# First chunk's heads: more idle products, one pair's softmax split over GpSimd and one exponential, the first weight's scaling placed earlier

## Chip, cores, metric

One core of a Trainium2 chip. The metric is the device time of one execution in microseconds (us); lower is better.

## What is computed

Attention over 8 batches, 8 heads, 576 positions and 64 dimensions, then a two-layer feed-forward block on the 4608 tokens. Heads 0 to 3 are local (a query sees the 32 keys up to its own position), heads 4 to 7 are strided (keys at the same position modulo 32).

```python
scores = scale * q @ k.T
scores = where(mask, scores, -1e9)
attn = exp(scores - max(scores)); attn /= sum(attn) + 1e-9
x = (attn @ v) -> [4608, 512]
h = maximum(x @ w_in, 0)            # w_in  [512, 2048]
out = (h * h) @ w_out               # w_out [2048, 512]
```

## The kernel before

The 4608 tokens go through in 12 chunks of 384. For each chunk TensorE does 16 steps of `up` (line 465: x times a slice of w_in, 12 products of 384 columns) and 16 steps of `down` (line 493: squared result times a slice of w_out, 9 products of 512 columns). To keep single precision, every operand is split into a high and a low part and three products stand for one.

**The start.** Before the first `up` the x of chunk 0 has to be there. Its eight heads are worked on in four pairs by `pe_pair` (line 295), a generator that the main code advances step by step: `first[0]` and `first[1]` are the two pairs of local heads, `late[0]` and `late[1]` the two pairs of strided ones. A pair goes through scores on TensorE (line 325), masked row minima on VectorE (line 330), exponentials on ScalarE, row sums and reciprocals on VectorE (lines 358, 359), the multiplication by the reciprocal (line 362), transposes on TensorE into the banks of the scores (line 368), copies to SBUF (lines 370, 372), the products with v (lines 380, 391), and the split into the x tiles (lines 395, 396).

**Two ways to the exponential.** The local pairs of chunk 0 (`single`) take eight exponentials of 128 columns, each with its own bias and row sum (line 353), from SBUF into the PSUM bank of the scores; ScalarE reads its accumulator out after each. All other pairs subtract the minima on GpSimd (line 355), take one exponential per head (line 356) and sum on VectorE (line 357).

**Idle products.** `zeros(bank, n)` issues n products of 128 columns whose result nobody reads: 60 at the very start, 45 after the scores of the first three pairs. The products of `first[0]` with v are issued three times over (line 378), to the same place. 12 more stand ahead of the first `down`.

**The weights.** `convert` (line 147) is a generator over the 16 weight blocks, in two halves each: a scaling of the raw block on ScalarE (`scale`, line 154), a step on ScalarE into PSUM bank 3 (line 166), one on VectorE (line 169), a copy of the high part on ScalarE (line 172) and a subtraction for the low part on GpSimd (line 173). `behind(ins, gen)` puts each instruction that gen issues behind the given instruction of the same engine. The first two steps are placed behind the last exponential of `first[1]`; the four that follow stand behind the last copy of the heads (line 395), and the others are spread between the `up` steps of chunk 0.

**Order.** The framework's planner places the traced instructions on each engine by its own estimate of time, with the order of the trace as priority; the engines then take them strictly in that order. While chunk 0 runs through `up` and `down`, GpSimd and VectorE also do chunk 1's strided heads by elementwise multiplications and reductions (`strided`, line 400), which begin behind the fifth weight subtraction.

Of the kernel before, what the change touches and what calls it, by code (L numbers as in the profile page):

```python
# [11 lines left out]
AF = mybir.ActivationFunctionType  # L12
ALU = mybir.AluOpType
AX = mybir.AxisListType
# [14 lines left out]
QC = 96  # L29
NW = TC // QC  # L30
# [8 lines left out]
NWARM = 60  # L39
# [10 lines left out]
def f32(ap):  # L50
    return ap.bitcast(F32)
# [11 lines left out]
def windows(c):  # L63

    res, at = [], 0
    for b, g in SEGS[c]:
        for qc in (2 * g, 2 * g + 1):
            if res and res[-1][:2] != (b, qc - 1):
                at += STR
            res.append((b, qc, at))  # L70
            at += QC
    return res
# [14 lines left out]
def attn_moe(ctx: ExitStack, tc, qk_l, v_l, qk_d, v_d, qk_p, v_p, f_s, q_s, k_s, v_s, w_in, w_out, masks, eye, out):  # L87
    nc = tc.nc
# [13 lines left out]
    def psum(i, nm):  # L102

        return ps.tile([P, 512], F32, name=nm, tag=f"ps{i}")
# [17 lines left out]
    last = {}  # L122
# [9 lines left out]
    def fetch(k):  # L132

        p, which = order[k]
        src = (w_out if which else w_in)[p].bitcast(U32).rearrange("p (n t) -> p n t", t=2)
        if k < 12:
            raw = wpool.tile([P, 1024, 2], U32, name=f"raw{k}", tag=f"w{k + 8 if k < 8 else k + 4}")
            nc.sync.dma_start(out=raw, in_=src)
            raws[k] = [(raw, slice(0, 1024))]
        else:  # L140
            raws[k] = []
            for i in range(0, 1024, WP):
                raw = spool.tile([P, WP, 2], U32, name=f"raw{k}_{i}", tag="s3", bufs=5)
                nc.sync.dma_start(out=raw, in_=src[:, i : i + WP])
                raws[k].append((raw, slice(i, i + WP)))

    def convert():

        split = None

        def scale(k):
            for raw, _ in raws[k]:

                nc.scalar.activation(f32(raw[:, :, 1]), f32(raw[:, :, 1]), AF.Prelu, scale=2.0**-112, alpha=-(2.0**32))  # L154

        scale(0)
        for k in range(NFT):
            p, which = order[k]
            t = wpool.tile([P, 2, 1024], F32R, name=f"w{which}_{p}", tag=f"w{k}")
            (wo if which else wi)[p] = t[:, 0], t[:, 1]  # L160
            cuts = [(raw[:, i : i + WP], sl.start + i) for raw, sl in raws.pop(k) for i in range(0, sl.stop - sl.start, WP)]
            for raw, at in cuts:

                z = psum(zbank[next(zturn) % len(zbank)], f"z{k}_{at}").bitcast(U32)
                w, hi, lo = raw[:, :, 1], t[:, 0, at : at + WP], t[:, 1, at : at + WP]
                first_step = nc.scalar.activation(z, raw[:, :, 0], AF.Copy, bias=-0.49, scale=2.0**-29 * (1 - 2.0**-9))  # L166
                if split:
                    split()
                last["v"] = nc.vector.scalar_tensor_tensor(out=w, in0=w, scalar=3, in1=z, op0=ALU.logical_shift_left, op1=ALU.bitwise_or)

                def split(w=w, hi=hi, lo=lo, at=at, k=k):
                    last["a"] = nc.scalar.copy(hi, f32(w))
                    last["g"] = nc.gpsimd.tensor_sub(lo, f32(w), f32(hi))  # L173
                    if at and 4 <= k < 12:
                        fetch(k + 4)

                if k == 0 and at:
                    split()
                    split = None
                if not at and k + 1 < NFT and k + 1 in raws:  # L180
                    with tc.issue_after(first_step.ins):
                        scale(k + 1)
                yield
        split()
# [110 lines left out]
    def pe_pair(c, pr, local, qk, vr, es, pt, banks, sm, single):  # L295
# [3 lines left out]
        if local:  # L299
            kw, wins, nv = KW, [at for _, _, at in windows(c)], P  # L300
            src, vsrc = qk_d[c, pr], v_d[c, pr]
            mk = [mask_sb[:QC, w % 2, :] for w in range(NW)]
        else:
            kw, wins, nv = QC, [QC * w for w in range(NW)], QC
# [9 lines left out]
        nm = small.tile([P, 2, NW], F32, name=f"nm{u}", tag="nm")  # L314
        rs = small.tile([P, 2, NW], F32, name=f"rs{u}", tag="rs")
        ss = sums[sm]
# [3 lines left out]
        e4 = [blocks(e) for e in es]  # L320

        r4 = [blocks(t) for t in s_ps] if single else e4
# [23 lines left out]
                minima(h, s)  # L346
        yield
        for h in range(2):
            if single:
                for w in range(NW):  # L350
                    if c == 0 and pr and h and not w:
                        yield
                    last["a"] = nc.scalar.activation(r4[h][:, w], e4[h][:, w], AF.Exp, bias=nm[:QC, h, w : w + 1], scale=-1.0, accum_out=ss[:QC, NW * h + w, :1])  # L353
            else:
                nc.gpsimd.tensor_sub(e4[h], e4[h], nm[:QC, h].unsqueeze(2).broadcast_to([QC, NW, kw]))  # L355
                last["a"] = nc.scalar.activation(e4[h], e4[h], AF.Exp, scale=-1.0)
                nc.vector.tensor_reduce(out=ss[:QC, NW * h : NW * (h + 1), 0], in_=e4[h], op=ALU.add, axis=AX.X)
        nc.vector.tensor_reduce(out=rs[:QC].rearrange("p h w -> p (h w)"), in_=ss[:QC], op=ALU.add, axis=AX.X)
        last["v"] = nc.vector.reciprocal(rs[:QC], rs[:QC])
# [4 lines left out]
        p4 = pt.rearrange("p (h w q) -> p h w q", h=2, w=NW)  # L364
        for h in range(2):
            t = s_ps[h] if s_ps else banks()
            for w in range(NW):
                nc.tensor.transpose(t[:kw, w * QC : (w + 1) * QC], e4[h][:, w], ident[:QC, :QC])
            if c == 0 and not local:
                nc.vector.tensor_copy(pt[:kw, h * TC : (h + 1) * TC], t[:kw, :TC])  # L370
            else:
                last["a"] = nc.scalar.copy(pt[:kw, h * TC : (h + 1) * TC], t[:kw, :TC])
# [148 lines left out]
    def behind(ins, gen):  # L521

        while True:
            with ExitStack() as st:
                for i in ins.values():
                    st.enter_context(tc.issue_after(i.ins))
                try:
                    k = next(gen)
                except StopIteration:
                    return  # L530
            yield k


    def pair_at(c, pr, local, place, psum_at):
        u = f"{c}_{pr}_{int(local)}"
        buf = lambda pl, nm, n, tag, **kw: pl.tile([P, n], F32, name=f"{nm}{u}", tag=tag, **kw)
        ee = lambda pl, tag: [buf(pl, f"e{h}", 512, tag) for h in range(2)]
        if place == 0:
            b = buf(lraw, "qk", TC + KC, "qk"), buf(lpool, "v", 512, "vx", bufs=1), ee(lpool, "e"), buf(lpool, "pt", 2 * TC, "px")
        elif place == 1:  # L540
            b = buf(lraw, "qk", TC + KC, "qk"), buf(ypool, "v", 512, "ysb"), ee(ypool, "ysb"), buf(lpool, "pt", 2 * TC, "px")
        elif place == 2:
            e = buf(xpool, "e", 2 * TC, "xlh")
            b = buf(xpool, "qk", 2 * TC, "xll"), buf(xpool, "v", 2 * TC, "xsl")[:, :512], [e[:, :TC], e[:, TC:]], buf(lpool, "pt", 2 * KC, "kx", bufs=1)[:, : 2 * TC]
        else:

            t = buf(wpool, "w", 2048, "w7")
            b = buf(xpool, "qk", 2 * TC, "xsh"), buf(spool, "v", 512, "s3", bufs=5), [t[:, :512], t[:, 512:1024]], t[:, 1024 : 1024 + 2 * TC]
        it = iter(range(10))

        def bank():
            i = next(it) % len(psum_at)
            if psum_at[i] == "y":
                return ps_y.tile([P, 512], F32, name=f"b{i}{u}", tag="psy")
            return psum(int(psum_at[i]), f"b{i}{u}")

        return pe_pair(c, pr, local, *b, bank, place % 3, c == 0 and local)
# [21 lines left out]
    def take(c, which):  # L579

        if NPLAIN <= c < NCHUNK:
            for h in map(int, which):
                if (c, h) not in heads:
                    heads[c, h] = pe_head(c, h)
                with ExitStack() as st:
# [4 lines left out]
                    last["pe"] = last.get("mm", last["pe"])  # L590

    ungated = convert()

    late = [pair_at(0, pr, False, 2 + pr, ("y0", "14")[pr]) for pr in range(2)]
# [7 lines left out]
    def zeros(bank, n):  # L602
        w_ps = psum(bank, f"w_ps{bank}")
        for _ in range(n):
            nc.tensor.matmul(w_ps[:, :P], warm, warm, start=True, stop=True)  # L605
# [17 lines left out]
        for k in range(NEARLY, 8):  # L623
            fetch(k)
    next(late[0])
    zeros(1, 3 * NWARM // 4)
    next(first[0])
    parts = last["v"], last["a"]
    with tc.issue_after(parts[1].ins):
# [4 lines left out]
    next(first[0])  # L634
    with tc.issue_after(last["a"].ins):
        next(first[1])
    weights = behind({"a": last["a"]}, ungated)
    next(first[1])
    next(late[1])
    for _ in range(2):  # L640
        next(weights)
    next(first[0])
# [4 lines left out]
    weights = behind({"a": last["a"]}, ungated)  # L647
# [6 lines left out]
    for s in range(NS + 2):  # L654
        c, j = divmod(s, NFT)
# [19 lines left out]
        if s < NFT - 2:  # L675

            weights = behind({"a": last["gh"]} | ({"x": last["xs"]} if s > NFT - 4 else {}), ungated)
# [108 lines left out]
```

## Time and profile before

| | us |
|---|---|
| median of 3 runs | 880.89 |
| lowest, highest | 880.71, 881.80 |
| profiled execution, its time | 881.58 |
| profiled execution, its span | 879.8 |
| outside the span | 1.8 |
| mean granted TensorE clock | 0.998 |

| engine | busy us | share of the span |
|---|---|---|
| TensorE | 869.2 | 99% |
| VectorE | 640.5 | 73% |
| ScalarE | 571.7 | 65% |
| GpSimd | 672.4 | 76% |

These shares are means over unlike stages: the start (up to 27.5 us), the `up` and `down` of chunk 0 beside the conversion of the weights (to 108 us), and eleven chunks in which TensorE has all it needs. In the views, PE is TensorE's products, PEld its weight loads, DVE VectorE, ACT ScalarE, POOL GpSimd.

### The profile page before, as it was taken

The page shows a single profiled execution, that of the slowest core. Times are in us where ns is not written, and L with a number is a line of the kernel's source. Part 1 is how long each engine was busy: PE and PEld are TensorE (multiplying, and loading weights), DVE is VectorE, ACT ScalarE, POOL GpSimd, SP SyncE. Part 2 cuts the span into 40 slices and gives each one's busy share as a digit, 9 for nine tenths or more (in the row PEclk, how much of TensorE's full clock was granted, in tenths as well). Part 3 has the DMA queues.
Part 4 walks back from the last instruction along what each step waited for, and adds up shares of the span by engine and source line. Part 5 has one row for each costly group of instructions (what it writes and reads, how often), then busy time and mean ns, then how long its engine had stood idle before and what let it go on. Part 6 is the DMA issues. An engine that isn't in the chain of part 4 may idle for free.

```text
span 879.8 us, 14906 instructions
## 1 busy us (share of the span) xinstructions
PE 869.2 (99%) x4773; PEld 790.0 (90%) x4773; DVE 640.5 (73%) x1900; ACT 571.7 (65%) x1506; POOL 672.4 (76%) x718
## 2 busy tenths in 40 slices
PE   8999999999999999999999999999999999999997
PEld 7788899999999999999999999999998989999996
DVE  5796687787787887878878778878787787883111
ACT  6999777586676566657657758657666665664332
POOL 3589778877988989888988978997998899782000
PEclk9999999999999999999999999999999999999999
DMA  9853531323123023112202302312131121000000
GB/s 356 356 199 107 163 101 39 101 84 113 31 78 111 26 89 103 44 51 85 67 13 80 115 13 74 97 38 75 31 102 57 32 71 61 6 1 12 26 1 36
DMA packets 26798, 71.41 MB, mean 81 GB/s; under 512 B 2976, under 2 KB 8736, under 8 KB 25184
## 3 DMA queue, kind: packets, MB, share of 16 engines
q1 hardware_dynamic: 26432, 70.14, 24.0%
q8 instruction: 37, 0.61, 0.3%
q14 instruction: 41, 0.34, 0.1%
q10 hardware_dynamic: 288, 0.33, 0.1%
HBM read 61.01 MB, written 9.44 MB: 80 GB/s over the span
## 4 chain that ended last, share of the span: by engine, by line
PE 90%; POOL 4%; ACT 2%; DVE 1%; DMA 1%; issue 1%; DVEq 0%; POOLq 0%; ACTq 0%
PE y L508 42%; PE h L475 42%; POOL w L173 2%; PE s L237 2%; PE o L283 2%; DMA raw<-w_out 1%; PE w_ps L605 1%; PE b L380 1%; ACT b L353 1%; ACT raw L154 1%; ACT z L166 0%; POOL pp L447 0%; DVE sc L432 0%; PE b L391 0%; POOL e L355 0%
## 5 line engine op out<-in xcount | busy, mean ns | idle before, releaser
L508 PE MATMUL y<-w,gh 128*128 128x512 f32 x1152 | 357.9, 391 | 0.5 <-POOL w L173 0.5
L508 PEld LDWEIGHTS y<-w,gh 128*128 128x128 f32 x1152 | 212.7, 188 | 40.5 <-POOL w L173 0.8
L475 PE MATMUL h<-xlh,w 128*128 128x384 f32 x768 | 229.1, 339 | 1.4 <-ACT xlh L395 0.9
L447 POOL TENSOR_TENSOR pp<-vs,sc 128x448 f32<-128x448 f32 (+10 forms) x192 | 189.9, 1013 | 48.9 <-DVE qs L448 23.0
L475 PE MATMUL h<-xsh,w 128*128 128x384 f32 x768 | 226.3, 335 | 0.3 <-POOL w L173 0.3
L508 PE MATMUL y<-w,gl 128*128 128x512 f32 x576 | 225.2, 392 | 0.0
L425 POOL TENSOR_TENSOR pq<-ks,qs 128x512 f32<-128x512 f32 (+2 forms) x192 | 197.7, 1050 | 18.6 <-DVE sc L426 13.2
L489 DVE TENSOR_TENSOR gl<-h,gh 128x384 fp32r<-128x384 f32 x192 | 105.5, 550 | 80.9 <-ACT gh L488 79.6
L488 ACT CAST gh<-h 128x384 fp32r<-128x384 f32 x192 | 91.3, 476 | 104.4 <-PE y L508 103.0
L486 ACT ACTIVATE h<-h 128x384 f32<-128x384 f32 x176 | 83.1, 472 | 110.0 <-PE h L475 109.5
L426 DVE TENSOR_REDUCE sc<-pq 128x8 f32<-128x512 f32 (+4 forms) x228 | 119.7, 534 | 45.3 <-POOL pq L425 42.6
L475 PEld LDWEIGHTS h<-xlh,w 128*128 128x128 f32 x768 | 141.3, 188 | 5.0 <-ACT xlh L395 1.1
L475 PEld LDWEIGHTS h<-xsh,w 128*128 128x128 f32 x768 | 141.4, 188 | 1.1 <-POOL w L173 0.6
L475 PE MATMUL h<-xll,w 128*128 128x384 f32 x384 | 129.0, 336 | 0.0
L508 PEld LDWEIGHTS y<-w,gl 128*128 128x128 f32 x576 | 108.1, 188 | 22.9
L475 PE MATMUL h<-xsl,w 128*128 128x384 f32 x384 | 128.3, 334 | 0.0
L448 DVE TENSOR_REDUCE qs<-pp 128x64 f32<-128x448 f32 (+11 forms) x192 | 106.4, 562 | 27.2 <-POOL pp L447 25.2
L487 ACT ACTIVATE h<-h 128x384 f32<-128x384 f32 x176 | 83.2, 473 | 3.6
L262 DVE STREAM_TRANSPOSE p_t<-e 32x128 f32<-32x128 f32 x240 | 72.3, 301 | 11.2 <-ACT e L251 6.6
L475 PEld LDWEIGHTS h<-xll,w 128*128 128x128 f32 x384 | 72.2, 188 | 2.4 <-DVE xll L396 0.3
L475 PEld LDWEIGHTS h<-xsl,w 128*128 128x128 f32 x384 | 72.1, 188 | 0.1
L246 ACT ACTIVATE e<-e,nm 96x128 f32<-96x128 f32 x160 | 62.5, 392 | 10.0 <-DVE nm L229 8.7
(101 smaller groups left out, 1077.2 us busy)
## 6 DMA issues: line engine op xcount, KB each, us to landing
qk<-qk_l SPq DMA_DIRECT2D x24, 400.0 KB, 3.2
y<-ysb SPq DMA_DIRECT2D x36, 256.0 KB, 3.5
raw<-w_in SPq DMA_DIRECT2D x7, 1024.0 KB, 10.9
qk<-qk_l SPq DMA_DIRECT2D x16, 416.0 KB, 3.2
vs<-v_s SPq DMA_DIRECT2D x10, 576.0 KB, 3.8
raw<-w_out SPq DMA_DIRECT2D x5, 1024.0 KB, 12.6
v<-v_l SPq DMA_DIRECT2D x40, 128.0 KB, 2.0
ks<-k_s SPq DMA_DIRECT2D x8, 576.0 KB, 3.7
```

Of the source, the lines that this page charges most:

```text
L246: nc.scalar.activation(e[:QC, cut(w)], e[:QC, cut(w)], AF.Exp, bias=nmax[:QC, w : w + 1], scale=-1.0, accum_out=ssum[:QC, w, :1])
L262: nc.vector.transpose(out=pt[STR * k : STR * (k + 1), :, STR * r : STR * (r + 1)], in_=e.rearrange("p (w k) -> p w k", k=KW)[STR * r : STR ...
L425: nc.gpsimd.tensor_mul(pv, kt[:, a : a + m, :], qt[:, i - i0 : i - i0 + 1, :].broadcast_to([P, m, D]))
L426: nc.vector.tensor_reduce(out=sc[:, i - i0, a : a + m], in_=pv, op=ALU.add, axis=AX.X)
L447: nc.gpsimd.tensor_mul(pv, vt[:, a : a + nd, :n], sc[:, il : il + 1, :n].broadcast_to([P, nd, n]))
L448: nc.vector.tensor_reduce(out=ot[:, il, a : a + nd], in_=pv, op=ALU.add, axis=AX.X)
L475: done = nc.tensor.matmul(ph[:, :TC], w[:, wsl], xx, start=n == 0, stop=n == 11)
L486: nc.scalar.activation(g, g, AF.Relu)
L487: nc.scalar.activation(g, g, AF.Square)
L488: last["gh"] = nc.scalar.copy(gh, g)
L489: nc.vector.tensor_sub(gl, g, f32(gh))
L508: done = nc.tensor.matmul(y_ps[c][t], g[:, sl], w[:, wsl], start=j == 0 and k == 0, stop=j == NFT - 1 and k == 2)
```

## The change

It does five things. (1) The second group of idle products has 55 instead of 45. (2) The four transposes of the second head of `first[0]` are issued twice, to the same place. (3) The second head of `first[1]` no longer takes four exponentials with accumulators: GpSimd subtracts the minima from all 512 columns, ScalarE takes one exponential of 512 columns into the PSUM bank, VectorE sums the rows out of it. (4) The scaling of the first weight block becomes a step of its own (a `yield` behind it), traced behind that exponential and ahead of the transposes of `first[1]` and the rest of `late[1]`. (5) The first two conversion steps proper are traced after that rest and stand behind `late[1]`'s first exponential on ScalarE (remembered as `a0`) and its last reciprocal on VectorE.

```diff
@@ convert
         scale(0)
+        yield
         for k in range(NFT):
@@ pe_pair
         for h in range(2):
-            if single:
+            if single and pr and h:
+
+                yield
+                nc.gpsimd.tensor_sub(e4[h], e4[h], nm[:QC, h].unsqueeze(2).broadcast_to([QC, NW, kw]))
+                last["a"] = nc.scalar.activation(r4[h], e4[h], AF.Exp, scale=-1.0)
+                nc.vector.tensor_reduce(out=ss[:QC, NW * h : NW * (h + 1), 0], in_=r4[h], op=ALU.add, axis=AX.X)
+            elif single:
                 for w in range(NW):
-                    if c == 0 and pr and h and not w:
-                        yield
                     last["a"] = nc.scalar.activation(r4[h][:, w], e4[h][:, w], AF.Exp, bias=nm[:QC, h, w : w + 1], scale=-1.0, accum_out=ss[:QC, NW * h + w, :1])
             else:
                 nc.gpsimd.tensor_sub(e4[h], e4[h], nm[:QC, h].unsqueeze(2).broadcast_to([QC, NW, kw]))
                 last["a"] = nc.scalar.activation(e4[h], e4[h], AF.Exp, scale=-1.0)
+                last["a0"] = last["a0" if h else "a"]
@@ pe_pair, transposes
-            for w in range(NW):
+
+            for w in [*range(NW)] * (2 if c == 0 and local and not pr and h else 1):
                 nc.tensor.transpose(t[:kw, w * QC : (w + 1) * QC], e4[h][:, w], ident[:QC, :QC])
@@ main
-    zeros(1, 3 * NWARM // 4)
+    zeros(1, NWARM - 5)
@@ main
     with tc.issue_after(last["a"].ins):
         next(first[1])
-    weights = behind({"a": last["a"]}, ungated)
+    next(behind({"a": last["a"]}, ungated))
     next(first[1])
     next(late[1])
+    weights = behind({"a": last["a0"], "v": last["v"]}, ungated)
     for _ in range(2):
         next(weights)
```

## Rows read from the trace of the kernel before

**Rows 1.** The page's chain that ended last, shares of the span by line.

```profile
PE y L508 42%; PE h L475 42%; POOL w L173 2%; PE s L237 2%; PE o L283 2%; DMA raw<-w_out 1%; PE w_ps L605 1%; PE b L380 1%; ACT b L353 1%; ACT raw L154 1%; ACT z L166 0%; POOL pp L447 0%; DVE sc L432 0%; PE b L391 0%; POOL e L355 0%
```

**Rows 2.** The same chain in order of time (start, length, what), the start.

```profile
15.97 4.22 PE b L380 x48
...
21.17 1.29 DVE e L362 x2
...
27.61 0.47 ACT xsh L395
```

**Rows 3.** Busy time by stretch: length, PE, PEld, DVE, ACT, POOL, clock, DMA share, GB/s.

```profile
14.00:16.00 2.00, 1.07 (x9) 0.76 (x9) 2.00 (x10) 2.00 (x8) 0.26 (x1) 1.00 1.03 430
16.00:18.00 2.00, 2.00 (x24) 1.82 (x26) 1.96 (x14) 1.63 (x7) 1.49 (x2) 0.63 1.00 410
18.00:20.00 2.00, 2.00 (x28) 2.00 (x24) 1.11 (x6) 2.00 (x6) 1.72 (x3) 0.51 1.01 422
20.00:22.00 2.00, 1.68 (x17) 1.22 (x17) 1.30 (x3) 2.00 (x4) 1.61 (x2) 1.00 1.04 422
22.00:24.00 2.00, 1.86 (x30) 1.58 (x30) 2.00 (x5) 1.51 (x4) 0.00 (x0) 1.00 0.98 410
...
32.00:36.00 4.00, 3.60 (x27) 2.84 (x26) 2.67 (x6) 4.00 (x8) 1.62 (x2) 1.00 1.03 407
```

**Rows 4.** TensorE in order of time, products and weight loads: start, length, what, [idle before].

```profile
9.86 2.69 PE L605 MATMUL w_ps<-p_t 128*128 128x128 bf16 x45
12.47 1.33 PE L325 MATMUL b<-qk 64*96 64x96 f32 x16
...
15.04 0.37 PEld L368 LDWEIGHTS b<-ident,e 96*128 96x128 f32 x4 [0.28 <-ACT e L356]
...
16.34 3.66 PEld L380 LDWEIGHTS b<-pt,v 128*64 128x64 f32 x46 [0.18 <-ACT pt L372]
...
25.24 0.69 PEld L380 LDWEIGHTS b<-pt,v 128*64 128x64 f32 x14
```

**Rows 5.** VectorE in order of time, the start.

```profile
15.30 0.24 DVE L330 CUSTOM_DVE_ANT_0 w<-b,mask_sb 96x96 f32<-96x96 f32 x1
...
18.90 0.55 DVE L357 TENSOR_REDUCE sums<-w 96x4 f32<-96x384 f32 x1 [0.77 <-ACT w L356]
...
20.70 0.55 DVE L370 COPY pt<-b 96x384 f32<-96x384 f32 x1 [0.81 <-PE b L368]
...
27.46 1.22 DVE L396 TENSOR_TENSOR xsl<-b,xsh 64x384 fp32r<-64x384 f32 x2
```

**Rows 6.** GpSimd in order of time.

```profile
12.66 1.61 POOL L355 TENSOR_TENSOR e<-e,nm 96x384 f32<-96x384 f32 x2 [9.81 <-DVE nm L330]
...
18.12 1.61 POOL L362 TENSOR_TENSOR e<-e,rs 96x384 f32<-96x384 f32 x2
...
45.09 5.21 POOL L173 TENSOR_TENSOR w<-raw,w 128x512 fp32r<-128x512 f32 x4
```

**Rows 7.** ScalarE in order of time, the start.

```profile
17.45 0.35 ACT L353 ACTIVATE b<-e,nm 96x128 f32<-96x128 f32 x1
...
17.96 0.37 ACT L353 ACTIVATE b<-e,nm 96x128 f32<-96x128 f32 x1
...
19.16 1.11 ACT L154 ACTIVATE raw<-raw 128x1024 f32<-128x1024 f32 x1
```

**Rows 8.** Lines by form, least/median/most ns (356, 357); landing of the first two weight loads.

```profile
L356 ACT ACTIVATE e<-e x6: 508/614/632, 14.2 to 79.5; 96x512 f32<-96x512 f32 x4, 96x384 f32<-96x384 f32 x2
...
L357 DVE TENSOR_REDUCE sums<-e x6: 539/676/684, 14.8 to 80.1; 96x4 f32<-96x512 f32 x4, 96x4 f32<-96x384 f32 x2
...
DMA to landing us min/median/max: 8.8/9.8/10.9
```

**Rows 9.** VectorE and TensorE in order of time, while chunk 0 runs.

```profile
47.07 3.29 DVE L432 TENSOR_TENSOR sc<-sc,mx 128x36 f32<-128x36 f32 x1
...
103.77 0.62 PE L475 MATMUL h<-xlh,w 128*128 128x384 f32 x2 [0.91 <-ACT xlh L395]
```

## The prediction

> **What bounds the kernel now.** I read the page's chain by line first: 84% of the span lies on the products of `up` and `down` [rows 1]. Everything the change touches lies before the first `up` at 27.5 us, so it can only let the same TensorE work begin sooner or later. Then the same chain in order of time. For the start it runs: the threefold products of `first[0]` with v, 4.22 us from 15.97; the transposes of `late[0]`; the multiplication of `first[1]` on VectorE, 1.29 us from 21.17; the rest of the pairs; the last x copy on ScalarE at 27.61 [rows 2]. Behind that copy the code places the third conversion step, so weights and first `up` both follow the end of the heads.
>
> [...] The weight loads give the pace: 46 of these products in 3.66 us, 0.080 each, while the same products of `first[1]` at full clock take 0.69 for 14, 0.049 each [rows 4].
>
> **Part by part.** *Ten more idle products.* 45 take 2.69 us, so ten take 0.60. The scores of `late[1]` behind them, 12.47 to 13.80, move to 13.07 to 14.40 [rows 4]. VectorE takes the first of their minima at 15.30, so 0.9 us cover it [rows 5]; without that cover it would cost the 0.6. The first transposes begin about 14.4, so the cost on TensorE is 0 to 0.05 us. They close the idle time between the scores and the transposes.
>
> *Four transposes twice.* Four take 0.37 us [rows 4]. They stand ahead of the copy of the second head, but that copy follows the one of the first head on ScalarE, so the delay is between 0 and 0.37; I take 0.2. Both edits fill the stretch from 13.8 to 16 in which TensorE was half idle [rows 3]. If the clock then stays up, 46 products gain 0.031 each, 1.4 us; less the 0.2, the threefold products end 1.2 us sooner, near 19.0. If it falls all the same, they end 0.2 later. The transposes of `late[0]` behind them need GpSimd's multiplication, whose first half is done at 18.12 + 0.80 = 18.9 [rows 6], so the 1.2 can be used.
>
> Do transposes hold the clock? From 20 to 24 TensorE ran almost nothing but transposes, busy 1.68 and 1.86 of each 2.00 us, and the clock stayed at 1.00 [rows 3]. [...]
>
> *One exponential for four.* Four small ones take 0.35 to 0.51 us each (0.51 from one at 17.45 to the next at 17.96 [rows 7]), 1.4 to 2.0 together; the one of 512 columns has 0.61 [rows 8]. ScalarE is relieved by 0.8 to 1.4; I take 1.2, less the 0.2 by which the exponential starts later, 1.0. GpSimd's subtraction: 1.61 us for two of 384 columns, so 1.07 for 512. GpSimd had sat idle for 9.81 us when its first subtraction began at 12.66 [rows 6], and these minima are done by 11.8; so it fits ahead, at worst pushing the others by 0.3, while ScalarE is still at other exponentials. Without that cover it costs 1.07. VectorE gets one more sum, 0.68 [rows 8]. That one is not free: VectorE is full in most of the stretch.
>
> *The multiplication of `first[1]`.* Its exponential now ends near 17.1 instead of 19.1. Before, the multiplication stood behind a copy that waited 0.81 us for the slow products and began at 20.70 [rows 5]. It can now come ahead of that copy, which takes up to 1.29 out of the chain, and nothing if the planner leaves it there.
>
> *The first scaling.* One ScalarE instruction, 1.11 us [rows 7], with no transfer of its own; its block was issued at 6.1 and lands at 14.9 by the shorter of the two landings, 8.8 [rows 8]. From about 17.1 it can run while ScalarE would wait for `late[1]`'s subtraction. `late[1]`'s exponentials queue behind it, as do copies of the pair; cost 0 to 1.1 for that pair. I take 0.3, as GpSimd hands over the second half only about 1.1 us after the scaling would start. The step after it now also waits on VectorE for `late[1]`'s reciprocal, with transposes' copies queued behind; before, that VectorE step ran only at 22.8, far later, so I cost it at nothing.
>
> *The sum.* Along the chain: 1.2 from the products, up to 1.3 from the multiplication, 2.5 together. That is more than the other two engines allow. VectorE was idle 0.89 from 18 to 20 and 0.70 from 20 to 22 [rows 3]; less the new sum that leaves 0.9. It ends with the last split at 27.46 + 1.22 = 28.68 [rows 5], with about 0.5 idle before it after 26, so at most 1.4. ScalarE's 1.0 and its idle 0.49 from 22 to 24 make 1.5. I take 1.2 us, with 0.6 and 1.9 as ends. What comes later follows: ScalarE is full from 32 to 36 with conversion [rows 3], begun behind the heads' last copy, and GpSimd's work for chunk 1 begins behind the fifth weight. The profiled execution, 879.8 of span and 1.8 around it, would give 881.58 - 1.2 = 880.4; it lies 0.7 above the median of the runs, so I predict 880.9 - 1.2 = 879.7.
>
> **Rivals.** *The clock falls all the same.* The products end 0.2 later; only the multiplication's place and ScalarE's relief are left, about 0.5: 880.4. For it: GpSimd and ScalarE still leave a gap before the first v product. Against: the stretch from 20 on.
>
> *The gain is swallowed.* TensorE waits 0.91 us at 103.77 for chunk 1's x [rows 9]; if the chain through GpSimd keeps its place, that wait grows by what the start gave: 880.9.
>
> *A held VectorE instruction falls better.* At 47.07 a subtraction of 36 elements takes 3.29 us and ends at 50.36, as GpSimd's run of four weight subtractions ends (45.09 + 5.21 = 50.30) [rows 6, 9]; the softmax of chunk 1's strided heads waits behind it. If the shift meets a shorter run, the chain through GpSimd is up to 3 us sooner and TensorE recovers its 0.91: 880.9 - 1.2 - 0.9 = 878.8. [...]
>
> *It falls worse (the slower side).* If the planner puts six subtractions in one run, 6 x 1.30 = 7.8 us, and that instruction comes at its start, it is held 4.5 us longer, GpSimd's chain follows, and TensorE waits for x at 104: 880.9 + 4.5 - 1.2 = 884.2. It decides against the change from 1.2 us of extra hold on. For it: everything after the start is planned anew. Against: a run of four is what the same rules gave.
>
> **Chances.** Forecast 0.44 (878.9 to 880.3); clock falls 0.16; swallowed 0.10; falls better 0.20 (877.5 to 879.1); falls worse 0.10 (881.5 to 884.2). What this kernel's measurement can tell from no change is about 0.2%, 1.8 us, so faster means below 879.1: nearly all of "falls better" and a third of the forecast, 0.32. Slower means above 882.7, most of "falls worse": 0.09. Within: 0.59. The range leaves out the outer parts of the two last cases: 877.3 to 882.2.
>
> **What would show it.** Right: clock 1.00 from 16 to 20 and 46 v products in about 2.3 us; one exponential of 512 columns near 16.5; `first[1]`'s multiplication before 20; the last x copy near 26.4 instead of 27.61; the first `up` moved alike. Wrong: a clock near 0.5 in that stretch; `late[1]` last by more than before; a gain at 27 that is gone at 108; or a time outside the range, which would mean that the planner's new order of chunk 0, not the start, decides.

## The result, and the profile after

| | before | after |
|---|---|---|
| median, us | 880.80 | 883.43 |
| lowest, highest, us | 880.34, 881.80 | 882.66, 884.64 |
| profiled execution, its time, us | 881.58 | 883.50 |
| profiled execution, its span, us | 879.8 | 881.7 |
| mean granted TensorE clock | 0.998 | 0.999 |

The ratio of after to before is 1.0035, interval 1.0025 to 1.0045: the change costs about 3.1 us by the ratio (2.6 by the medians), where 1.2 us of gain was forecast and the range ended at 882.2.

Lines moved: 605 is now 612, 325 is 326, 353 (small exponentials) 358, 355 to 357 are 360, 361, 363, 358 and 359 are 364 and 365, 362 is 368, 368 is 375, 370 is 377, 372 is 379, 380 is 387, 391 is 398, 395 and 396 are 402 and 403, 173 is 174, 432 is 439, 475 is 482, 488 and 489 are 495 and 496, 508 is 515. The new subtraction, exponential and sum are 353, 354 and 355.

**What came as forecast.** The stretches of after (columns as in [rows 3]) show the clock held:

```profile
16.00:18.00 2.00, 1.74 (x28) 1.44 (x28) 2.00 (x20) 1.30 (x3) 1.01 (x2) 1.00 0.99 406
18.00:20.00 2.00, 1.96 (x38) 1.57 (x33) 1.90 (x5) 2.00 (x4) 2.00 (x3) 1.00 1.00 418
20.00:22.00 2.00, 1.20 (x12) 1.01 (x12) 2.00 (x7) 2.00 (x5) 0.17 (x1) 1.00 1.04 426
```

It was 0.63 and 0.51 from 16 to 20 [rows 3]. The weight loads of the same kernel give the pace of the threefold products, and show `late[1]`'s scores (line 326) ahead of them and TensorE's wait for the last v products:

```profile
14.94 0.75 PEld L326 LDWEIGHTS b<-qk 64*96 64x96 f32 x8
...
17.23 2.01 PEld L387 LDWEIGHTS b<-pt,v 128*64 128x64 f32 x46 [0.45 <-ACT pt L379]
...
26.94 1.29 PEld L398 LDWEIGHTS b<-w,v 96*32 96x32 f32 x30 [0.79 <-DVE w L377]
```

46 loads take 2.01 us instead of 3.66 [rows 4]. They start 0.9 later and still end near 19.2 instead of 20.0. ScalarE waits 0.72 us for the transposes of `first[0]`'s second head, has its one exponential of 512 columns at 17.08, and the scaling comes right behind it:

```profile
16.70 0.48 ACT L379 COPY pt<-b 128x384 f32<-128x384 f32 x1 [0.72 <-PE b L375]
17.08 0.60 ACT L354 ACTIVATE b<-e 96x512 f32<-96x512 f32 x1
17.61 1.17 ACT L154 ACTIVATE raw<-raw 128x1024 f32<-128x1024 f32 x1
18.67 0.92 ACT L361 ACTIVATE w<-w 96x384 f32<-96x384 f32 x2
...
28.49 0.48 ACT L402 CAST xsh<-b 64x384 fp32r<-64x384 f32 x1 [0.19 <-PE b L398]
```

The last of these is the last x copy: 28.49, not 26.4; before it was at 27.61 [rows 2]. Every step that was forecast as a gain is there, and yet the heads end 0.9 us later (0.82 counted from the first row minimum).

**Where the heads lost it.** GpSimd of after, in order of time:

```profile
12.01 1.04 POOL L353 TENSOR_TENSOR e<-e,nm 96x512 f32<-96x512 f32 x1 [9.17 <-DVE nm L331]
...
18.56 1.61 POOL L368 TENSOR_TENSOR e<-e,rs 96x384 f32<-96x384 f32 x2
22.79 1.61 POOL L368 TENSOR_TENSOR w<-w,rs 96x384 f32<-96x384 f32 x2 [2.62 <-DVE rs L365]
```

The new subtraction is free, as costed. The last line is `late[1]`'s multiplication by its reciprocal. Before, the same line stood at 20.03, 0.30 us behind `late[0]`'s (18.12 + 1.61 = 19.73 [rows 6]), as its reciprocal on VectorE began at 19.57. VectorE's line, then GpSimd's, of before:

```profile
19.57 0.31 DVE L359 RECIPROCAL rs<-rs 96x8 f32<-96x8 f32 x2
```

```profile
20.03 1.61 POOL L362 TENSOR_TENSOR w<-w,rs 96x384 f32<-96x384 f32 x2 [0.30 <-DVE rs L359]
```

Now GpSimd idles 2.62 us for that reciprocal. VectorE of after, over that time:

```profile
17.73 0.67 DVE L355 TENSOR_REDUCE sums<-b 96x4 f32<-96x512 f32 x1
...
18.86 1.28 DVE L368 TENSOR_TENSOR e<-b,rs 96x512 f32<-96x512 f32 x2
20.07 0.99 DVE L363 TENSOR_REDUCE sums<-w 96x4 f32<-96x384 f32 x2
20.99 1.00 DVE L377 COPY pt<-b 96x384 f32<-96x384 f32 x2
21.92 0.15 DVE L364 TENSOR_REDUCE rs<-sums 96x8 f32<-96x16 f32 x1
21.99 0.54 DVE L403 TENSOR_TENSOR xll<-b,xlh 128x384 fp32r<-128x384 f32 x1
22.46 0.18 DVE L365 RECIPROCAL rs<-rs 96x8 f32<-96x8 f32 x1
```

`first[1]`'s multiplication has indeed left its place behind the copy (18.86 instead of 21.17). But it and the new sum now stand ahead of `late[1]`'s row sums (20.07, both; before, they ran at 17.57 and 18.90 [rows 5]), and `late[0]`'s copies and the split of `first[0]` ahead of `late[1]`'s reciprocal, which VectorE starts only at 22.46, the last of these lines. `late[1]` is now the last pair.

**Behind the heads.** TensorE's weight loads with the longest waits from 36 to 155 us, after:

```profile
36.65 1.22 PEld L515 LDWEIGHTS y<-w,gh 128*128 128x128 f32 x6 [0.55 <-ACT gh L495]
...
45.08 0.30 PEld L482 LDWEIGHTS h<-xlh,w 128*128 128x128 f32 x2 [1.86 <-POOL w L174]
...
105.03 0.30 PEld L482 LDWEIGHTS h<-xlh,w 128*128 128x128 f32 x2 [0.77 <-ACT xlh L402]
...
115.28 0.19 PEld L482 LDWEIGHTS h<-xlh,w 128*128 128x128 f32 x1 [0.23 <-DVE gl L496]
...
124.58 0.19 PEld L482 LDWEIGHTS h<-xlh,w 128*128 128x128 f32 x1 [0.57 <-DVE rs L248]
...
151.77 0.19 PEld L482 LDWEIGHTS h<-xlh,w 128*128 128x128 f32 x1 [0.51 <-DVE gl L496]
```

and before:

```profile
40.99 0.19 PEld L475 LDWEIGHTS h<-xlh,w 128*128 128x128 f32 x1 [0.87 <-ACT w L172]
42.11 0.19 PEld L508 LDWEIGHTS y<-w,gh 128*128 128x128 f32 x1 [0.82 <-POOL w L173]
...
103.77 0.30 PEld L475 LDWEIGHTS h<-xlh,w 128*128 128x128 f32 x2 [1.09 <-ACT xlh L395]
...
107.92 0.48 PEld L237 LDWEIGHTS s<-kx,qx 128*96 128x96 f32 x4 [0.83 <-POOL qx L223]
```

From 36 to 46 us after waits 0.55 + 1.86 = 2.41 where before waits 1.69. Around 105 it waits 1.15 less (0.77 against 1.09 + 0.83). In chunk 1 it waits three times, 1.31 together, where before has no wait above 0.15 us. On balance these make about 0.9 us more; summed over all waits above 0.15 us from 29 to 160 us it is 7.40 against 6.92, 0.5 us more. The VectorE instruction that took 3.29 us [rows 9] takes 0.30, which goes with the relief at 105:

```profile
46.05 0.30 DVE L439 TENSOR_TENSOR sc<-sc,mx 128x36 f32<-128x36 f32 x1
```

The planner had put chunk 0 and chunk 1 in another order on all engines. There are two losses, then, one in the heads and one behind them.

### The profile page after: what moved, and what is told of

It reads as the page before. It is cut to its first block, busy times and chain, and to the rows that moved or that the text cites. A ratio compares the mean times of both kernels' runs of the same rounds, so it can differ in the third digit from the quotient of the medians.

```text
span 881.7 us, 14939 instructions
## 1 busy us (share of the span) xinstructions
PE 869.7 (99%) x4787; PEld 789.9 (90%) x4787; DVE 639.3 (73%) x1901; ACT 569.0 (65%) x1499; POOL 673.9 (76%) x719
## 4 chain that ended last, share of the span: by engine, by line
PE 87%; POOL 4%; DVE 3%; ACT 3%; DMA 1%; issue 1%; DVEq 0%; POOLq 0%; ACTq 0%
PE h L482 41%; PE y L515 41%; PE s L238 2%; PE o L284 2%; POOL pq L432 1%; POOL w L174 1%; DMA raw<-w_out 1%; PE w_ps L612 1%; PE b L326 1%; ACT b L358 1%; DVE p_t L263 1%; POOL pp L454 0%; ACT z L167 0%; ACT raw L154 0%; DVE sc L433 0%
```

## The experiments

Where the texts on record name theories by letters: **A** is that the loss arises in the heads, with `late[1]` made last; **A1** puts that down to the early scaling ahead of its exponentials on ScalarE, **A2** to VectorE's order; **B** is that the new order of chunks 0 and 1 costs time by itself.

Two readings of each run stand in the table. The end of the last x copy is counted from the first row minimum on VectorE, because that minimum itself comes at 7.45 to 8.77 us from trace to trace (last section); before it is 19.68 us, after 20.50. "Order behind" says whether the planner's order behind the heads is that of the kernel before. The last column takes the heads' shift off what the ratio makes of 880.7 us; by the ratio's interval each of its figures is uncertain by about 0.9 us (1.2 to 1.3 in e4 and e5).

| kernel | median us | ratio to before | heads end, us against before | order behind | rest, us |
|---|---|---|---|---|---|
| after | 883.43 | 1.0035 (1.0025 to 1.0045) | +0.82 | new | 2.3 |
| e1, idle products and transposes only | 879.92 | 0.9994 (0.9985 to 1.0004) | -0.62 | before's | 0.1 |
| e2, softmax split only | 881.98 | 1.0017 (1.0008 to 1.0026) | +1.22 | before's | 0.3 |
| e3, early scaling only | 882.58 | 1.0023 (1.0014 to 1.0032) | +1.26 | before's | 0.8 |
| e4, all but the early scaling | 883.24 | 1.0036 (1.0021 to 1.0051) | +2.46 | new, of its own | 0.7 |
| e5, `late[1]` traced first | 884.97 | 1.0049 (1.0035 to 1.0063) | +3.78 | before's | 0.5 |
| e6, scaling later | 883.12 | 1.0035 (1.0025 to 1.0045) | +0.50 | after's | 2.6 |
| e7, one more idle product | 882.58 | 1.0022 (1.0013 to 1.0031) | +0.80 | new, of its own | 1.1 |
| e8, all but the idle work | 882.53 | 1.0024 (1.0014 to 1.0034) | +0.50 | after's | 1.6 |
| e9, reciprocal first | 880.40 | 0.9996 (0.9987 to 1.0005) | -0.61 | before's | 0.3 |
| e10, new sum left out | 880.21 | 0.9992 (0.9983 to 1.0000) | -0.66 | before's | 0.0 |
| e11, e1 and reciprocal first | 880.59 | 0.9999 (0.9990 to 1.0009) | -0.60 | before's | 0.5 |
| e12, after's start, before's order behind | 881.84 | 1.0012 (1.0002 to 1.0021) | +0.81 | before's | 0.3 |

### One part alone: e1, e2, e3

The kernel before with one part of the change each. e1:

```diff
-    zeros(1, 3 * NWARM // 4)
+    zeros(1, NWARM - 5)
-            for w in range(NW):
+            for w in [*range(NW)] * (2 if c == 0 and local and not pr and h else 1):
```

> The kernel before with the idle products alone (55 instead of 45, four transposes twice); exponentials and scaling as before. Theory A (the strided pair late[1] is made last by the other parts; idle products only hold the clock): granted clock 1.00 from 16 to 20 us, threefold products end near 19.3 instead of 20.2, last x copy on ScalarE at 27.0 or sooner (27.61 before), time 880.8 - 0.6 = 880.2, not above 880.8. Theory B (every new build gets a new order for the rest of chunk 0 and chunk 1, and that order decides): the last x copy sooner in the same way, but the time anywhere between 879 and 883, set by waits of TensorE after 30 us that do not follow the start.

e2 has the subtraction, the one exponential and the sum of `first[1]`'s second head; e3 has the `yield` behind `scale(0)` and the later conversion steps.

> The kernel before with the softmax of the second head of first[1] split over GpSimd, one exponential and a sum on VectorE; idle products and scaling as before. Theory A: first[1] is done sooner but late[1]'s reciprocal and GpSimd multiplication come later than before (multiplication from 20.0 to 21 or later), clock low from 16.5 to 20 as before; last x copy at 27.6 to 28.6; time 881 to 882.5. Theory B: the time does not follow the last x copy; the shift of TensorE's products at 160 us differs from the shift of the first up by over 1 us.

> The kernel before with the first scaling as a step of its own and the first two conversion steps placed behind late[1]'s first exponential and last reciprocal; exponentials and idle products as before. Theory A: the scaling still stands behind the fourth small exponential, so it cannot get ahead of late[1]'s exponentials as it does in the changed kernel; late[1] keeps its place, last x copy within 0.4 of 27.61, time 880.4 to 881.4. Theory B: as likely 2 us away from it as not.

e1 is the only part that makes the heads end sooner, by 0.62. Its clock row for 16 to 18 reads 1.00, that of e2 0.50:

```profile
16.00:18.00 2.00, 1.74 (x26) 1.45 (x27) 1.88 (x19) 1.00 (x5) 0.94 (x2) 1.00 0.98 397
```

```profile
16.00:18.00 2.00, 2.00 (x28) 2.00 (x28) 1.93 (x14) 2.00 (x4) 1.62 (x3) 0.50 1.03 422
```

(e1 first, then e2; columns as in [rows 3].) The time of e1 can't be told from before. Both other parts alone make `late[1]` late. GpSimd of e2, then of e3:

```profile
23.57 1.61 POOL L368 TENSOR_TENSOR w<-w,rs 96x384 f32<-96x384 f32 x2 [0.43 <-DVE rs L365]
```

```profile
22.27 1.61 POOL L368 TENSOR_TENSOR w<-w,rs 96x384 f32<-96x384 f32 x2 [2.51 <-ACT xlh L402]
```

From the first minimum these start at 15.77 and 13.84 us; before it is 11.63. In e3 there is no new sum at all: there the reciprocal stands behind `late[0]`'s copies, for which VectorE waits 1.24 us. ScalarE's order changed as well, against the expectation: the last small exponential of `first[1]` runs behind a conversion step and a scaling, at 20.38 instead of 18.77, so `first[1]` is later too. What of this ended the heads was not tried. VectorE of e3:

```profile
20.72 1.02 DVE L377 COPY pt<-b 96x384 f32<-96x384 f32 x2 [1.24 <-PE b L375]
21.66 0.23 DVE L364 TENSOR_REDUCE rs<-sums 96x8 f32<-96x16 f32 x2
21.84 0.28 DVE L365 RECIPROCAL rs<-rs 96x8 f32<-96x8 f32 x2
```

The losses do not add: +1.22, +1.26 and -0.62 make +1.86, and the whole change has +0.82.

### Is it the scaling? e4, e6

e4 is the changed kernel with the scaling and the first two conversion steps placed as before, behind the last exponential of `first[1]`. In e6 the scaling is traced later, behind `first[1]`'s next step and the rest of `late[1]`:

```diff
-    next(behind({"a": last["a"]}, ungated))
     next(first[1])
     next(late[1])
+    next(behind({"a": last["a"]}, ungated))
```

> The changed kernel without its scaling part: the first two conversion steps stand behind the new exponential together, as in the kernel before. Theory A, in the form that the scaling ahead of late[1]'s exponentials costs the 0.9 us at the end of the heads: last x copy near 27.0 to 27.6 if only the scaling is to blame, near 28.5 as in the changed kernel if it is the new sum and the multiplication of first[1] ahead of late[1]'s sums on VectorE; time 881 or 883.4. Theory B: time unrelated to the last x copy.

> The changed kernel with the first scaling placed behind late[1]'s second exponential instead of ahead of the first; all else as in the changed kernel, and nearly the same planned order. Theory A1 (the scaling on ScalarE ahead of late[1]'s exponentials delays late[1]): multiplication of late[1] at 21.5 or sooner, last x copy at 27.6 or sooner, time near 882. Theory A2 (VectorE's queue delays it: first[1]'s sum and multiplication ahead of late[1]'s sums, late[0]'s copies ahead of late[1]'s reciprocal): multiplication at 22.5 to 23, last x copy 28.3 to 28.7, time 883 to 884.

In e4 a conversion step and the second scaling come between `late[1]`'s two exponentials (the first scaling stands ahead of both, at 17.54). The second exponential is only at 20.61, and GpSimd's multiplication at 24.70 (16.30 from the first minimum), later than either form of the expectation had it:

```profile
18.61 0.51 ACT L361 ACTIVATE w<-w 96x384 f32<-96x384 f32 x1
19.02 0.61 ACT L167 ACTIVATE z<-raw 128x512 uint32<-128x512 uint32 x1
19.58 1.15 ACT L154 ACTIVATE raw<-raw 128x1024 f32<-128x1024 f32 x1
20.61 0.52 ACT L361 ACTIVATE w<-w 96x384 f32<-96x384 f32 x1
```

So, for the heads, part (5), the conversion steps placed behind `late[1]`, is needed once (3) is there; the time of e4 can't be told from after's. In e6 the first of `late[1]`'s exponentials runs ahead of the scaling, and the multiplication starts 14.29 us behind the first minimum; with the scaling ahead it is 14.32. Theory A1 falls: in the changed kernel the scaling's place costs `late[1]`'s multiplication nothing, as VectorE's queue is later still. The heads of e6 do end 0.3 us sooner than after's. Behind that multiplication TensorE takes eight products with v sooner there and VectorE a split later; which of it gives the 0.3 was not tried.

### Other places for `late[1]`, other idle work: e5, e7, e8

e5 traces `late[1]`'s exponentials, sums and reciprocal ahead of `first[1]`'s; e7 is the changed kernel with 56 idle products; e8 has 45 and the transposes once.

> The changed kernel with late[1]'s subtraction, exponentials, sums and multiplication traced ahead of first[1]'s second head, and the first scaling behind late[1]'s second exponential; nothing is left out. In the planned order VectorE takes late[1]'s sums ahead of first[1]'s multiplication, and the order of everything after the start is that of the kernel before. Theory A (late[1]'s place in VectorE's queue decides the end of the heads, and the rest follows): late[1]'s multiplication on GpSimd starts near 20.5 (22.79 in the changed kernel), last x copy at 26.6 to 27.2, TensorE's products at 112 us and at the end are both 0.5 to 1.5 sooner than before, time 879.3 to 880.3. Theory that the new exponential or its sum costs by itself: not below 881.

> The changed kernel with 56 idle products instead of 55. One product more is 0.06 us; the start keeps the order of the changed kernel, the planner's order of the rest differs from it in some tens of places. Theory A alone: the same time within 0.3, 883.1 to 883.7, last x copy 28.5. Theory B (the order of chunk 0 and 1 adds its own 1 to 2 us): last x copy 28.5, but the shift between 112 us and the end, 1.2 in the changed kernel, changes by over 0.4.

> The changed kernel without its idle products (45 products, four transposes once). Theory A: the threefold products run at the low clock, late[0]'s copies on VectorE wait for them, late[1]'s multiplication 22.5 or later, last x copy at 28.5 to 29.5, time 883 to 884.5. Theory B: time set by the order of the rest, which here differs from that of the kernel before in hundreds of places as in the changed kernel; shift from 112 us to the end over 0.5.

e5 missed its expectation and moved the fault: `late[1]`'s multiplication came at 12.97 us from the first minimum, and `first[1]`'s went behind four things at once (two copies, a conversion step and a split) and became the last:

```profile
22.18 0.50 DVE L377 COPY pt<-b 96x384 f32<-96x384 f32 x1
22.60 0.54 DVE L403 TENSOR_TENSOR xll<-b,xlh 128x384 fp32r<-128x384 f32 x1
23.06 1.27 DVE L368 TENSOR_TENSOR e<-b,rs 96x512 f32<-96x512 f32 x2
```

e7 changed the order behind the heads once more with a single idle product, and nothing else of the start; its time can't be told from after's. e8 says what the held clock was worth in the changed kernel. Its weight loads:

```profile
16.28 3.66 PEld L387 LDWEIGHTS b<-pt,v 128*64 128x64 f32 x46 [0.18 <-ACT pt L379]
```

The products are slow again, as before (the clock reads 0.60 and 0.54 from 16 to 20), and yet its heads end 0.3 us sooner than after's (later was expected), with `late[1]`'s multiplication at 14.30. In the changed kernel, where `late[1]` waits for VectorE, the faster products bought nothing.

### VectorE's order: e9, e10, e11

e9 is the changed kernel with `late[0]`'s copies and `first[0]`'s split behind `late[1]`'s reciprocal on VectorE, all work kept:

```diff
-    weights = behind({"a": last["a0"], "v": last["v"]}, ungated)
+    lr = last["v"]; weights = behind({"a": last["a0"], "v": lr}, ungated)
...
-    next(first[0])
+    with tc.issue_after(lr.ins): next(first[0])
...
-        next(late[0])
+        with tc.issue_after(lr.ins): next(late[0])
```

> The changed kernel, all of it, but the copies of late[0]'s transposed scores and the split of first[0] stand on VectorE behind the reciprocal of late[1], where the changed kernel has them ahead of it. Nothing is left out of the computation. Theory A2 (VectorE's order made late[1] last): late[1]'s multiplication on GpSimd starts about 1.4 us sooner than in the changed kernel (12.9 us after the first minimum instead of 14.3), the last x copy 0.5 to 1.0 us sooner, and with the order of chunk 0 and 1 that goes with it there is no loss between 112 us and the end (theory B): 881.0 to 881.8 us. If late[1] is late for another reason (the scaling on ScalarE), the multiplication does not move: 882.5 to 883.5. The copies that now stand later may make TensorE wait for them instead (a new last one): then the multiplication is sooner and the last x copy is not, about 882.5.

e10 leaves out the new sum (line 355); e11 is e1 with `late[1]`'s sums and reciprocal ahead of `first[1]`'s, and `late[0]`'s copies behind that reciprocal.

> The changed kernel without VectorE's new sum of 512 columns: the row sums of the second head of first[1] are left out of the computation. It tells the price of that one instruction on VectorE from the price of the order around it. Theory A2: late[1]'s multiplication starts about 0.7 us sooner than in the changed kernel (13.6 us after the first minimum instead of 14.3), the last x copy 0.3 to 0.7 sooner; its order of chunk 0 and 1 is that of the kernel before, so by theory B nothing is lost behind 112 us: 881.0 to 882.0 us. If the order within the start is what counts and not the sum's length, the multiplication moves by less than 0.2 and the last x copy stays: 882.0 or so by theory B alone, 883.4 if B is wrong.

> The two edits on TensorE alone (ten more idle products, four transposes twice) on the kernel before, and late[1]'s reciprocal placed on VectorE ahead of the sums of first[1] and the copies of late[0]. Nothing is left out of the computation. Theory A2: what is left of the gain in the first experiment was held by late[1]'s multiplication, which started at 20.80; it now starts near 19.9, the last x copy 0.3 to 0.8 sooner than there, 879.2 to 879.8 us. If first[1] is last there and not late[1], its sums behind the reciprocal cost as much as they give: 879.9 to 880.8.

VectorE of e9:

```profile
20.21 1.00 DVE L363 TENSOR_REDUCE sums<-w 96x4 f32<-96x384 f32 x2
21.25 0.17 DVE L364 TENSOR_REDUCE rs<-sums 96x8 f32<-96x16 f32 x1
21.45 0.20 DVE L365 RECIPROCAL rs<-rs 96x8 f32<-96x8 f32 x1
```

The reciprocal follows the sums at once, the multiplication starts at 13.18 us from the first minimum (1.14 sooner than in after; 1.4 was expected), the heads end 1.43 sooner than after's (0.5 to 1.0 was expected), and the planner went back to the old order behind them. The whole change with three lines for one queue gives a ratio of 0.9996, where without them it gives 1.0035. That is A2, as far as the multiplication goes: only VectorE's order was prescribed. The planner then also moved `late[1]`'s transposes up on TensorE and two conversion instructions on ScalarE, so of the 1.43 only the 1.14 is shown to come from VectorE's queue. The time is slightly better than expected, since 881.0 was the lower end.

e10 starts the multiplication 1.97 us sooner than after (12.35), more than the sum's 0.67, because the queue changed with it (so it doesn't give that instruction's price), but its heads end only 0.05 sooner than e9's. In e11 the multiplication is at 11.86, 0.4 sooner than in e1, and the heads end where e1's do: the expected 0.3 to 0.8 did not come, which was the other case of its expectation. e1, e9, e10 and e11 lie within 0.06 us of each other at the heads' end, with `late[1]` ready anywhere from 11.86 to 13.18. So from about 13.2 on downwards something else ends the heads. In e10 it is the last v products, for which ScalarE waits ahead of each copy:

```profile
25.39 0.47 ACT L402 CAST xsh<-b 64x384 fp32r<-64x384 f32 x1 [0.24 <-PE b L398]
26.05 0.48 ACT L402 CAST xsh<-b 64x384 fp32r<-64x384 f32 x1 [0.19 <-PE b L398]
```

In e1 TensorE is busy for 2.00 of 2.00 us from 22 to 24 and from 24 to 26, so its own work may be that bound; this was not tried.

### The order behind the heads: e12

Three more idle products at the very start make the planner take the old order behind the heads, while up to the last x copy every engine has the changed kernel's order.

```diff
-    zeros(0, NWARM)
+    zeros(0, NWARM + 3)
```

> The changed kernel with 63 instead of 60 idle products at the very start. Nothing is left out of the computation. The planner then puts the instructions of the start in the same order on every engine as in the changed kernel, up to the last x copy and the first up, but the rest of chunks 0 and 1 in the order of the kernel before. It tells theory B from A2. If the order behind the heads costs what the traces of the changed kernel suggest (B): the last x copy 0.6 to 1.0 us later after the first minimum than in the kernel before (19.8 to 20.2 us behind it, as in the changed kernel), no wait of TensorE in chunk 1 that the kernel before does not have, and 881.3 to 882.0 us. If the late heads alone make the loss, it stays with the start unchanged: 883.2 to 883.8. If the downstream order of the kernel before swallows the late heads altogether: 880.6 to 881.2.

GpSimd, ScalarE and TensorE's weight loads of e12:

```profile
22.18 1.61 POOL L368 TENSOR_TENSOR w<-w,rs 96x384 f32<-96x384 f32 x2 [2.62 <-DVE rs L365]
```

```profile
27.87 0.48 ACT L402 CAST xsh<-b 64x384 fp32r<-64x384 f32 x1 [0.19 <-PE b L398]
```

```profile
101.91 0.19 PEld L482 LDWEIGHTS h<-xlh,w 128*128 128x128 f32 x1 [0.44 <-DVE gl L496]
```

The heads are the changed kernel's to 0.01 us: multiplication at 14.32, end at 20.49 (20.50 in after). Behind them the wait of 1.86 at 45 and the three of chunk 1 are gone, before's two of 0.87 and 0.82 are back (0.89 and 0.82, at 41 and 42); a wait of 0.44 at 102 is new. The relief around 105 is gone too (1.10 and 0.82).

The ratio is 1.0012 (1.0002 to 1.0021), and its interval does not meet that of after (1.0025 to 1.0045). So both theories hold: the late heads cost about 1 us, the new order behind them the other 2 (about 1.2 either way, an estimate from the two intervals). The last column of the table says the same over all runs: eight kernels with the old order have 0.0 to 0.8 us beside the heads' shift, the three with after's order 1.6 to 2.6; e4 and e7, each with an order of its own, have 0.7 and 1.1.

By the traces alone the size is smaller: from the last x copy to the last product of `down`, after takes 0.8 us more than before, e12 0.4 more. Over all traces this stretch is 1.0 us shorter to 0.4 longer than before's with the old order, 0.4 to 1.2 longer with after's, and behind that product after takes another 0.2 (4.90 against 4.68). The direction is shown, the size lies between 0.4 and 2. Which of the waits carries it was not tried.

## Why the prediction was wrong

Two steps failed: the multiplication of `first[1]` was taken as a gain with no price for what stands behind it, and the sum let all later work follow the heads in its old order.

**Clock and threefold products: right, a size off.** The clock held with the ten products and four transposes (1.00; e1 alone too), and without them it fell (e2 0.50, e8 0.60, both from 16 to 18; in e8 the products took 3.66 us). Which of the two held it was not tried, and with them eight of `late[1]`'s scores moved into that stretch as well (14.94). 46 products gave 1.65 us where 1.4 was worked out. But the delay put at 0.2 was 0.9: TensorE's queue has `late[1]`'s scores between the two heads' transposes, and ScalarE waited 0.72 for the second. About 0.8 of the 1.2 was left.

The prediction's reading of 20 to 24 before is half wrong: of the products that start from 20 to 22, 13 of 15 are transposes, but from 22 to 24 only 11 of 27, and the rest are products with v. Cleaner is 20 to 22 in after: the 12 products of the row are transposes, busy 1.20 us, behind a stretch with products at a clock of 1.00 (18 to 20), and the clock reads 1.00. The row shows that these did not lower the clock; no run here shows whether transposes alone would raise or hold it.

**One exponential, GpSimd's subtraction: right.** 0.60 us, at 17.08 instead of 16.5 because of the late copy ahead of it; the subtraction 1.04 us under cover.

**`first[1]`'s multiplication: the step that failed.** "It can now come ahead of that copy, which takes up to 1.29 out of the chain". It came 2.3 us sooner, and took nothing out, because the text asked only who waits for it and not who stands behind it in VectorE's queue: `late[1]`'s row sums and reciprocal, pushed back by the new sum (0.67), by this multiplication (1.28), and by copies and a split (1.54) that got ahead as well. 2.7 us later on GpSimd, `late[1]` became the last pair. The cap on the sum was counted from VectorE's idle time ("that leaves 0.9"), which says how much work fits into a stretch and nothing on the order in which it is taken. e9 keeps all the work, changes the order, and has no loss: the order made it.

**The scaling.** 0.3 was taken as its cost to `late[1]`. Both exponentials of `late[1]` do end later (19.59 instead of 18.87), but VectorE's queue hid that: moved behind the first of them (e6), the scaling leaves the multiplication where it was. Alone, without the other parts, parts (4) and (5) cost the heads 1.26 (e3), with VectorE's and ScalarE's order changed.

**The sum.** 1.2 sooner was forecast for the heads. In the four kernels whose `late[1]` is multiplied by 13.2 us behind the first minimum (e1, e9, e10, e11) it is 0.6, and the time lies within what can't be told from no change. The sum went on with "What comes later follows": that step failed as well, since the work behind the heads was put in another order, with the loss that e12 takes away.

**Rivals.** The slower side had its cause right in kind ("everything after the start is planned anew") and wrong in place: the VectorE instruction of 3.29 us fell better, with 0.30, and TensorE waited 1.15 us less around 105, about the 0.9 of "A held VectorE instruction falls better". But new waits at 37, 45 and in chunk 1 took 2.0 more. That a run of GpSimd's subtractions holds that VectorE instruction, on which both rivals were built, was not shown: in after it takes its 0.30, at 46.05, while GpSimd is at three of them (line 174, 3.86 us from 43.73). Both rivals followed one wait through the new order and took the others as they were. The better side did occur without a new order: in e1 and e9 the same instruction takes 0.65 and 0.72 us (3.19 to 3.25 in the other six with before's order), and their stretch from the last x copy to the last product of `down` is the shortest of these eight, 1.0 and 0.7 us less than before's. The slower side's chance of 0.10 was too low, since "a run of four is what the same rules gave" speaks for the order of before only; one idle product more (e7), or three (e12), was enough for another order. That another pair could become the last one was named as a sign at the end of the text and had no chance or price of its own: it should have been the first rival.

## What to carry to other kernels

When an instruction is moved up in an engine's queue, list what now stands behind it and who waits for that; idle time of an engine says that work fits, not that it comes in the right order. Where a planner orders later work by its own estimates, a small edit at the start can reorder everything behind it: compare the planned order of both kernels first, and try the edit with the old order kept, as a loss of 2 us may belong to the order and not to the edit. Work that keeps a clock up (here 1.00 from 16 to 20 us, where it read 0.63 and 0.51) is worth its price only as long as the products that it speeds up are on the last chain.

## What the runs showed that was not expected

The 60 idle products at the very start take a different time in each trace, 4.81 to 6.13 us, with nothing changed ahead of them. After, then e7:

```profile
1.56 5.83 PE L612 MATMUL w_ps<-p_t 128*128 128x128 bf16 x60 [1.56 <-POOL sums L120]
```

```profile
1.56 4.81 PE L612 MATMUL w_ps<-p_t 128*128 128x128 bf16 x60 [1.56 <-POOL sums L120]
```

From 4 to 6 us, 21 products start in after and 36 in e7, with a granted clock of 1.00 in the row of both; the second group of 45 takes 0.060 us each [rows 4], 21 in 2.00 us are 0.095 each. So the moment at which products reach the second group's pace at the start differs by about 1 us between these two traces (5.83 against 4.81), and with it the first minimum (7.45 to 8.77 over the 14 traces) and all that follows. It is as large as the effects looked for here, so the starts of two traces must be counted from an event behind it.
